# A fused adaLN attention and MLP block on one core: rearranging the prologue and the end of the kernel together

## The chip, the cores and the metric

The kernel runs on one core of one Trainium2 chip. The metric is the device time in microseconds of one execution. Each profile shows one execution; PE is the matrix engine (TensorE), ACT is ScalarE, DVE is VectorE, POOL is GpSimd, SP is SyncE, which only issues DMAs here.

An execution can differ from another by the clock that PE is granted. The trace records it: in the fast executions told here it is 1.00 except in windows of 0.50, whose lengths are multiples of 3.41 us. A run whose time is over 1.5% above the fastest of the same kernel is called slow and left out of comparisons.

## The reference

The inputs are bf16: x is 2048 x 640, there are 32 heads of 20, and the MLP is 1536 wide.

```python
mod = (silu(c) @ w_mod).reshape(1, 6, 1, 640)      # sa, ca, ga, sb, cb, gb
h = layernorm(x) * (1 + ca) + sa
x = x + ga * attention(h, wqkv, wo)                # softmax over 2048 keys
h = layernorm(x) * (1 + cb) + sb
x = x + gb * mlp(h)                                # mlp: layernorm, w1, gelu(tanh), w2
```

## The kernel before

The program is a list of operations, each with an engine, operands, an assumed duration and a priority. A list scheduler in the Python code plays a model of the chip and fixes, before anything runs, the order in which each engine gets its instructions. On the chip each engine takes its instructions strictly in this order. **A changed duration, threshold or DMA estimate in the model therefore changes the order of everything after it.**

The work has three parts. In the prologue the inputs are loaded, x is normalised and transposed, and the first projections are made. In the middle ACT computes 755 exps of 1024 or 1536 columns of scores and one shorter one, PE makes scores and sums, and DVE computes some scores' exps in its own way. Projections, the output projection, the second layer norm and the MLP of earlier query chunks are placed between. In the end the last chunk of 256 tokens does its layer norms and MLP with nothing left to hide behind.

**Filler.** PE is kept busy by matmuls with a zero weight matrix, which change no result. They are put where the modelled PE has a gap and the columns of the last modelled 3.4 to 4.4 us are below a threshold:

```python
class Sched:
    TICK = 3.413
    def __init__(self, nc, es):
        self.fill_min = 4500
        # ...
    def schedule(self):
        # ... bt: when the next PE operation could start, f0: when PE is free
                room = bt > f0 + 0.06
                while room and fl and fl[0][0] < min(bt, f0 + 1.0) - self.TICK:
                    fl.pop(0)
                if burst[1] or room and (bt > f0 + 1.5 and f0 > 30.0 or sum(x[1] for x in fl) < self.fill_min):
                    # ... a filler of up to 512 columns goes to PE
```

**Prologue.** Two small loads for the first head group come from ACT's queue; ACT copies their columns apart; a whole 512-column K block is projected before Q.

```python
for w in (1, 0):
    dma("act", raw0[:, w, :, :], wqkv_v[:, :, w * D:w * D + 80], 102400, prio=0)
dma("sp", wm0[:, :, 0:D], wmod_v[:, :, 0:D], 819200)
# ... stats, rstd (on GpSimd), normalize per token tile, transposes, then
proj_job(0, 1, tc, 0, eng="dve" if tc else "act")       # K
if tc == 0:
    proj_job(0, 0, tc, 0)                               # Q
```

The scheduler marks some operations with `lock`, meaning that GpSimd and DVE may not hold their common SBUF port at once. A GpSimd operation without an input, as a memset is, gets no lock:

```python
def pool(emit, W, R=(), dur=0.2, prio=5, name=""):
    return P.op("pool", emit, R=list(R), W=list(W), dur=dur, lat=dur + 0.12, prio=prio, name=name,
                lock=bool(R))
# ...
pool(lambda e: e.memset(wo_pad, 0.0), [wo_pad], dur=4.4, prio=7)
```

**End.** The softmax sums of the last head group are spread by a selecting matmul to 128 x 256, inverted by DVE in two pieces, and multiplied in. The second layer norm uses DVE for statistics, GpSimd for the inverse root, ACT for the normalise, DVE for the multiply and the add, and the same again for the MLP's own layer norm.

```python
sel_job(ci, NG - 1, prio=1, step=128)   # matmul, then per 128 columns: reciprocal, multiply
# ... last output matmul per half, wo_evac
def ln2(ci, tl, tail=False):
    stats(xt, tt, tl, 3)
    rstd(tt, 1, 1)                       # two GpSimd operations, a third in normalize
    normalize(hd, xt, tt, 3, on_act=tail)
    for op, row in ((ALU.mult, cb1), (ALU.add, sbr)):
        dve(lambda e, op=op, row=row: e.tensor_tensor(hd, hd, row, op=op), ...)
    stats(hd, tt, tl, 3, so=4); rstd(tt, 1, 1, so=4)
    normalize(hd, hd, tt, 3, so=4, on_act=tail)
```

The softmax here doesn't subtract the row's maximum and nothing guards it: scores larger than these inputs give would overflow.

## Time and profile before

| | before |
|---|---|
| timed runs, us | 967.31 median of 3 (966.62 to 972.41) |
| profiled execution, us | 1271.3, granted clock 0.556: a slow one |

The profile was of a slow execution. It shows what waits for what, but not what binds the timed runs.

The first fence is from the page of before: the span, busy time by engine, PE's granted clock in 40 slices (in tenths), the shares of the chain that ended last, and two of the costliest groups (busy us, mean ns, then the idle time before them).

```profile
span 1271.3 us, 17791 instructions
...
PE 1243.1 (98%) x7616; PEld 369.1 (29%) x7676; DVE 706.5 (56%) x1225; ACT 946.8 (74%) x804; POOL 152.0 (12%) x196
...
PEclk6555555555555555555555555555555555555555
...
PE 95%; DVE 3%; issue 1%; ACT 1%; DMA 0%; ACTq 0%
...
L739 ACT ACTIVATE arena<-psum 128x1536 bf16<-128x1536 f32 (+1 forms) x756 | 896.5, 1225 | 255.9 <-PE psum L730 247.2
...
L562 PE MATMUL psum<-arena 128*128 128x512 bf16 (+2 forms) x690 | 254.1, 482 | 0.5 <-issue 0.5
```

Line 739 is the exp, line 562 the filler (690 of them). PE was at about half clock all the time and was the bound of this execution.

The second fence is the timeline of before at its start: start, duration, engine, line, operation, output and input, count, and in brackets the idle time before it and what ended that.

```profile
0.73 3.77 ACTq L471 DMA_DIRECT2D arena<-in_A_wqkv_dram  x2
...
4.52 1.28 ACT L457 ACT_TABLE_LOAD   x1 [4.52 <-DMA arena<-in_A_wqkv_dram]
...
6.03 0.17 DVE L583 CAST arena<-psum 128x5 f32<-128x5 bf16 x1 [4.07 <-ACT arena L457]
...
6.45 0.48 DVE L614 BATCH_NORM_STATS2 arena<-arena 128x6 f32<-128x320 bf16 x1
...
23.61 1.02 ACT L739 ACTIVATE arena<-psum 128x1024 bf16<-128x1024 f32 x1 [1.98 <-PE psum L730]
```

ACT spends its first 4.5 us on issuing two loads, and the statistics of x stand behind ACT's tanh. The first exp starts at 23.61 in this slow execution.

The third is the timeline of before at its end.

```profile
1214.83 0.42 DVE L805 CAST arena<-psum 128x256 bf16<-128x256 f32 x1 [3.76 <-PE psum L797]
...
1216.48 1.77 DVE L816 RECIPROCAL arena<-psum 128x128 f32<-128x128 f32 x2 [1.23 <-PE psum L476]
...
1231.74 1.82 ACT L457 ACTIVATE arena<-arena 128x640 bf16<-128x640 bf16 x2 [3.89 <-POOL arena L628]
```

From the end of the last sums' copy (1215.25) to the end of the second normalised tile (1233.56) are 18.3 us.

### The profile page before, as it was taken

To read this page: it belongs to the slowest core of one execution; us is meant where nothing else is said; L and a number is where in the kernel's file an instruction comes from. 1 tells how busy PE (TensorE), PEld (TensorE's weight loads), DVE (VectorE), ACT (ScalarE), POOL (GpSimd) and SP (SyncE) were. 2 spreads that over 40 slices of the span, in tenths; PEclk is the share of its full clock that TensorE was granted. 3 is DMA by queue.
4 is the path that set the end of the run, shared out by engine and by line. 5 is a ranking of instruction groups with operands and counts; after the bars stand their busy time and mean duration, and the time that the engine had idled before them with its cause. 6 is when DMAs were issued, how large, how long until landed. Compare 5 with 4: busy or idle time off the path is not lost.

```text
span 1271.3 us, 17791 instructions
## 1 busy us (share of the span) xinstructions
PE 1243.1 (98%) x7616; PEld 369.1 (29%) x7676; DVE 706.5 (56%) x1225; ACT 946.8 (74%) x804; POOL 152.0 (12%) x196
## 2 busy tenths in 40 slices
PE   8999999999999999999999999999999999999999
PEld 3423222222222222222222222222233233333345
DVE  6522544554667766766567666666666543666030
ACT  3577777777778777887887877877778786888722
POOL 4200003000001251000013100000033000110010
PEclk6555555555555555555555555555555555555555
DMA  6200001100000030000000000100000000000000
GB/s 224 78 9 1 10 9 61 30 10 9 2 9 9 27 116 9 30 3 18 19 9 10 9 9 9 40 5 16 20 14 10 17 8 16 21 10 10 15 6 11
DMA packets 31521, 30.15 MB, mean 24 GB/s; under 512 B 12882, under 2 KB 26450, under 8 KB 31442
## 3 DMA queue, kind: packets, MB, share of 16 engines
q1 hardware_dynamic: 30130, 28.81, 7.1%
q8 instruction: 60, 0.98, 0.3%
q10 hardware_dynamic: 1312, 0.20, 0.1%
q14 instruction: 19, 0.16, 0.0%
HBM read 26.00 MB, written 2.88 MB: 23 GB/s over the span
## 4 chain that ended last, share of the span: by engine, by line
PE 95%; DVE 3%; issue 1%; ACT 1%; DMA 0%; ACTq 0%
PE psum L476 32%; PE psum L730 23%; PE psum L562 17%; PE psum L797 16%; PE psum L764 4%; PE psum L482 1%; ACT arena L739 1%; DVE arena L632 0%; DVE arena L614 0%; DVE arena L674 0%; DMA arena<-in_A_wqkv_dram 0%; DVE arena L1076 0%; DVE arena L805 0%; DVE arena L679 0%; DVE arena L661 0%
## 5 line engine op out<-in xcount | busy, mean ns | idle before, releaser
L739 ACT ACTIVATE arena<-psum 128x1536 bf16<-128x1536 f32 (+1 forms) x756 | 896.5, 1225 | 255.9 <-PE psum L730 247.2
L476 PE MATMUL psum<-arena 128*128 128x320 bf16 (+4 forms) x1643 | 467.1, 409 | 9.3 <-issue 5.9
L730 PE MATMUL psum<-arena 32*128 32x512 bf16 (+1 forms) x2339 | 380.6, 414 | 9.1 <-issue 5.9
L562 PE MATMUL psum<-arena 128*128 128x512 bf16 (+2 forms) x690 | 254.1, 482 | 0.5 <-issue 0.5
L797 PE MATMUL psum<-arena 128*32 128x512 bf16 (+3 forms) x2560 | 249.4, 415 | 0.6 <-DVE arena L805 0.4
L476 PEld LDWEIGHTS psum<-arena 128*128 128x128 bf16 (+1 forms) x1703 | 154.5, 112 | 239.8 <-issue 176.2
L776 DVE TENSOR_SCALAR arena<-psum 128x512 f32<-128x512 uint16 x176 | 121.5, 690 | 180.6 <-PE psum L764 150.5
L730 PEld LDWEIGHTS psum<-arena 32*128 32x128 bf16 x2339 | 78.9, 92 | 303.7 <-issue 173.7
L841 POOL TENSOR_TENSOR arena<-arena 128x512 bf16<-128x512 bf16 (+1 forms) x39 | 37.9, 973 | 837.1 <-DMA arena<-scr 837.0
L780 DVE SCALAR_TENSOR_TENSOR arena<-arena,psum 128x512 uint16<-128x512 f32 x176 | 120.1, 682 | 25.7 <-PE psum L797 21.7
L777 DVE TENSOR_TENSOR arena<-psum,arena 128x512 f32<-128x512 uint16 x176 | 120.9, 687 | 4.3
L778 DVE SCALAR_TENSOR_TENSOR arena<-psum,arena 128x512 f32<-128x512 uint16 x176 | 120.7, 686 | 3.6
L797 PEld LDWEIGHTS psum<-arena 128*32 128x32 bf16 (+1 forms) x2560 | 53.3, 92 | 178.4 <-issue 170.3
L562 PEld LDWEIGHTS psum<-arena 128*128 128x128 bf16 x690 | 68.2, 113 | 113.0 <-issue 101.1
L764 PE MATMUL psum<-arena 32*128 32x512 bf16 (+1 forms) x221 | 86.1, 423 | 1.9 <-DVE arena L679 0.4
L679 DVE TENSOR_SCALAR arena<-psum,arena 128x512 bf16<-128x512 f32 x31 | 23.2, 749 | 58.1 <-PE psum L476 44.6
L1076 DVE TENSOR_SCALAR arena<-psum,arena 128x512 bf16<-128x512 f32 (+1 forms) x48 | 32.8, 683 | 40.4 <-PE psum L476 38.5
L1097 DVE TENSOR_TENSOR arena<-psum,arena 128x320 bf16<-128x320 f32 x32 | 15.6, 489 | 64.0 <-PE psum L476 61.1
L674 DVE TENSOR_SCALAR arena<-psum,arena 128x512 bf16<-128x512 f32 x32 | 24.0, 751 | 45.1 <-PE psum L476 36.8
L805 DVE CAST arena<-psum 128x512 bf16<-128x512 f32 (+1 forms) x40 | 23.3, 584 | 44.7 <-PE psum L797 44.4
L614 DVE BATCH_NORM_STATS2 arena<-arena 128x6 f32<-128x320 bf16 x96 | 44.2, 478 | 0.3
L1056 POOL TENSOR_TENSOR arena<-arena 128x640 bf16<-128x640 bf16 x28 | 39.0, 1395 | 22.6 <-DVE arena L632 21.6
(54 smaller groups left out, 276.1 us busy)
## 6 DMA issues: line engine op xcount, KB each, us to landing
arena<-scr SPq DMA_DIRECT2D x24, 256.0 KB
arena<-in_A_x_dram SPq DMA_DIRECT2D x6, 640.0 KB, 11.5
arena<-in_B_w_dram SPq DMA_DIRECT2D x2, 1920.0 KB, 13.4
arena<-in_w_mod_dram SPq DMA_DIRECT2D x2, 1600.0 KB
out_dram<-arena SPq DMA_DIRECT2D x16, 160.0 KB, 1.8
arena<-in_A_wqkv_dram SPq DMA_DIRECT2D x3, 800.0 KB
arena<-scr SPq DMA_DIRECT2D x15, 128.0 KB
arena<-in_w_mod_dram SPq DMA_DIRECT2D x2, 800.0 KB
```

Source lines behind the costliest of these rows:

```text
L476: return P.op("pe", lambda e: e.matmul(outp, lhsT, rhs, start=start, stop=stop), R=[lhsT, rhs], W=[outp], dur=d, lat=d + 0.17, prio=prio, ...
L562: return lambda e: e.matmul(bank(b_)[:, 0:n_], zero, r_, start=new, stop=new, skip_group_check=True)
L614: dve(lambda e, hf=hf, xi=xi: e.bn_stats(s6[:, hf, :], xi), [xi], [s6[:, hf, :]], 320, prio=prio, dur=0.39)
L730: r = e.matmul(o_, lh, rh, start=True, stop=True, tile_position=(32 * hl, 0))
L739: acts.append(P.op("act", lambda e: e.activation(dst, pb, ACTF.Exp, scale=ESC, bias=EBIAS), R=[pb], W=[dst], dur=d, lat=d + 0.24, prio=4, ...
L764: r = e.matmul(o_, lh, rh, start=True, stop=True, tile_position=(32 * hl, 0))
L776: dve(lambda e: e.tensor_scalar_add(w_, m_, -65536.0), [pb], [w_], w, prio=1, name="d1", dur=0.6)
L777: dve(lambda e: e.tensor_tensor(w_, m_, w_, op=ALU.mult), [pb, w_], [w_], w, prio=1, name="d2", dur=0.6)
L778: dve(lambda e: e.scalar_tensor_tensor(out=w_, in0=m_, scalar=c2, in1=w_, op0=ALU.add, op1=ALU.mult), [pb, w_], [w_], w, prio=1, name="d3" ...
L780: dve(lambda e: e.scalar_tensor_tensor(out=o_, in0=w_, scalar=al, in1=pb, op0=ALU.mult, op1=ALU.add), [w_, pb], [o_], w, prio=1, name="d4" ...
L797: r = e.matmul(o_, lh, rh, start=(kt == 0), stop=(kt == TT - 1), tile_position=(0, 32 * hl))
L1056: pool(lambda e, op=op, row=row: e.tensor_tensor(hd, hd, row, op=op), [hd], [hd, row], dur=1.4)
```

## The change

The change starts the first exp earlier and shortens the end. The diff, cut to its core:

```diff
@@ scheduler
-        self.fill_min = 4500
+        self.fill_min = 5000
+        self.fill_all = 16.0
-                if burst[1] or room and (bt > f0 + 1.5 and f0 > 30.0 or sum(x[1] for x in fl) < self.fill_min):
+                if burst[1] or room and (bt > f0 + 1.5 and f0 > 30.0 or f0 < self.fill_all
+                                         or sum(x[1] for x in fl) < self.fill_min):
-                s = max(bt + 1.4, bw)
-                bw = s + o.nbytes / 350e3
-                o.t1 = bw + 0.6
+                big = o.nbytes > 65536
+                s = max(bt + (2.0 if big else 1.4), bw)
+                bw = s + o.nbytes / (330e3 if bt < 20.0 else 350e3)
+                o.t1 = bw + (1.6 if big else 0.6)
@@ prologue
-        for w in (1, 0):
-            dma("act", raw0[:, w, :, :], wqkv_v[:, :, w * D:w * D + 80], 102400, prio=0)
         dma("sp", wm0[:, :, 0:D], ...)
         dma("sp", wm0[:, :, D:2 * D], ...)
+        for w in (1, 0):
+            dma("sp", raw0[:, w, :, :], wqkv_v[:, :, w * D:w * D + 80], 102400)
-            act(dst, src, ACTF.Copy, n=400, prio=1)
+            pool(lambda e, dst=dst, src=src: e.tensor_copy(dst, src), [dst], [src], dur=0.5, prio=1)
-                    ["act", "dve", "dve"] if tc else ["act", "dve", "act"])      # who evacuates transposes
+                    ["act", "dve", "dve"])
-            proj_job(0, 1, tc, 0, eng="dve" if tc else "act")
             if tc == 0:
-                proj_job(0, 0, tc, 0)
+                proj_job(0, 1, 0, 0, eng="act", part=(0, 128))
+                proj_job(0, 0, 0, 0)
+                proj_job(0, 1, 0, 0, eng="act", part=(128, 512))
+            else:
+                proj_job(0, 1, tc, 0)
@@ end
+        act(rsm[:, 16:17], kcol[:, 0:1], ACTF.Sqrt, n=1, prio=9, name="table")
-        sel_job(ci, NG - 1, prio=1, step=128)
+        inv_tail(ci, NG - 1, inv, bankh(4))
+        #   transpose ot to token-major, reciprocal of its 8 sum columns, split the result in two bf16
+        #   parts, and spread them back with 16 small matmuls against the identity
-            ln2(ci, tl, tail=True)
+        a, b = (ln2_tail(ci, tl) for tl in range(nt))
+        #   one fixed DVE order (each operation follows the one before):
+        #   stats; ACT sqrt; (x - m) * cb1; reciprocal; x * r + sbr; stats; ACT sqrt; reciprocal; normalise
+        act(rsm[:, 17:18], ..., ACTF.Gelu_apprx_tanh, n=1, prio=2, name="table")
```

The rise of the filler threshold from 4500 to 5000 holds for the whole kernel.

## The prediction

> **What bounds the kernel now.** Timed median 967.31 us. The profiled execution is a slow one: span 1271.3 us, granted clock 0.556 (cores view), PE busy 98%, chain of waits 95% PE; so it shows the order of work, not the bound of the timed runs. At that clock 512 columns take 0.40 us back to back though PE never rests; the Trainium skill ("TensorE: Matmul & The Clock Gate", Part 1) says that a busy PE is released to full clock: this trace disagrees. At full clock I estimate PE work at 1243 x 0.556 = 690 us, so the timed runs should be bound by ScalarE: 947 us busy on the page, neighbours overlapping by some 0.1 us (three 1024-wide exps took 2.97, one alone 1.02). With 755 exps that leaves 870 to 910 us from first exp to last, and about 58 us for prologue and end. Only these two change.
>
> **Prologue.** First exp at 23.6 us (timeline). The chain of waits begins with two loads issued from ScalarE's queue (0.73 to 4.50), then the table load (1.28), tanh, and VectorE's small cast at 6.03, behind which the statistics stand until 6.45. The change issues these loads from SyncE, later. Statistics can start when x lands, about 4.5: 2 us. ScalarE evacuates two transposed tiles instead of three (3 took 2.11): 0.6 us. Only 128 columns of K before Q: 5 x 384 columns off the path to the first score, 0.8 us at full clock. Filling all PE gaps before 16 us (PE busy 2.16 of 4 in 8 to 12) may spare half-clock projections: 0 to 1.5 us. The weight copies move to GpSimd, off the path if their loads land by 11. Sum 4; perhaps 3 reach the end, since ScalarE still waits on other work up to 60 us.
>
> **End.** From the sums' copy (ends 1215.25) to the second normalised tile (1233.56): 18.3 us, estimated 16.3 at full clock (28 early output matmuls held PE). Now: two 128-column reciprocals (0.93 each), divides, per tile statistics, three GpSimd steps (0.22 + 0.55 + 0.27), ScalarE normalise (0.92), multiply and add (0.48 each), and statistics to normalise again. The change: reciprocal of 8 columns, two small ops, two short PE passes: 1 us less. The layer norms become one VectorE order: 4 evacuations 0.42, 8 statistics 0.42, 4 aggregates 0.12, 4 reciprocals 0.15, 4 fused scalar-tensor-tensor at (640 + 151)/0.96 = 0.82 (formula of "VectorE: DVE Perf Modes", errata section; the trace's 0.489 at 320 columns agrees), 2 normalises 0.4: 10.5, plus 1.8 before: 12.3. Gain 4. Tables (1.28 each) load ahead: at most 0.5, since PE bounds the following matmuls. Transposes, MLP and store (about 25 us at full clock) stay.
>
> **Sum.** 967.3 - 3 - 4.5 = 959.8 us; 80% range 953 to 965.5. Faster by over 2% (below 948): 0.05. Within 2%: 0.93. Slower: 0.02.
>
> **Signs.** Right: first statistics near 4.5, first exp at least 3 us earlier; 12 to 13 us from the sums' copy to the second normalised tile; no GpSimd in the end; exps unchanged. Wrong: GpSimd's copies or the late loads release the first K projection; fused ops over 0.9 us; a table load on the chain; first to last exp grows by what the prologue saved.
>
> **What would make it wrong.** More filler (5000 columns a window) delaying exps in the middle; a half-clock end in the timed runs too, where surplus fillers (20 us here) enlarge the saving; the early start absorbed before 60 us.

## The result, and the profile after

| | before | after |
|---|---|---|
| timed runs, us | 966.96 median of 4 (966.22 to 972.41) | 981.53 median of 4 (981.0 to 982.03) |
| ratio of fast runs | | 1.0138, 95% interval 1.0101 to 1.0176 |

A ratio is the mean time of one kernel's fast runs over that of the other's fast runs of the same rounds, so it is not quite the ratio of the medians. The kernel became 1.4% slower where I had predicted 0.8% faster. The interval lies wholly above 1.

The profile of after is of a fast execution. The same parts of its page:

```profile
span 979.2 us, 18273 instructions
...
PE 956.1 (98%) x7888; PEld 346.5 (35%) x7888; DVE 701.7 (72%) x1233; ACT 916.1 (94%) x807; POOL 149.8 (15%) x186
...
PEclk9799999999999999999999999999999999999999
...
PE 86%; ACT 8%; DVE 5%; issue 0%; POOL 0%; POOLq 0%; DVEq 0%
...
L747 ACT ACTIVATE arena<-psum 128x1536 bf16<-128x1536 f32 (+1 forms) x756 | 865.5, 1237 | 21.9 <-PE psum L738 16.0
...
L575 PE MATMUL psum<-arena 128*128 128x512 bf16 (+2 forms) x878 | 232.0, 357 | 0.0
```

Even at full clock the chain is 86% PE, and there are 878 fillers where there were 690. One slice has clock 7. What this has to be compared with is the chain of before, profiled later (before_fast), and its filler line:

```profile
ACT 45%; PE 42%; DVE 6%; DMA 3%; issue 1%; POOL 1%; SPq 0%; DVEq 0%
...
L562 PE MATMUL psum<-arena 128*128 128x512 bf16 (+2 forms) x690 | 177.1, 351 | 0.2 <-issue 0.2
```

So in fast executions the chain went from ACT and PE in about equal parts to nearly PE alone, and the filler's busy time from 177.1 to 232.0 us. The timeline of after at its start:

```profile
0.72 1.28 ACT L465 ACT_TABLE_LOAD   x1 [0.72 <-PEq L1288]
...
3.06 1.28 ACT L465 ACT_TABLE_LOAD   x1
...
4.91 1.67 DVE L627 BATCH_NORM_STATS2 arena<-arena 128x6 f32<-128x320 bf16 x4
...
17.74 1.28 ACT L747 ACT_TABLE_LOAD   x1
...
19.04 1.94 ACT L747 ACTIVATE arena<-psum 128x1024 bf16<-128x1024 f32 x2
```

The statistics start at 4.91, as predicted. There are two table loads more than expected (without the dummy square root, in after_no_table, only the one at 0.72 is left before the first exp). The dummy square root, meant to load a table ahead of the end, depends on nothing late. The scheduler put it at 4.70 us, and so the exp table had to be loaded again at 17.74, right before the first exp. The timeline at its end:

```profile
946.41 0.42 DVE L813 CAST arena<-psum 128x256 bf16<-128x256 f32 x1 [2.98 <-PE psum L805]
...
947.42 0.21 DVE L822 RECIPROCAL arena<-psum 128x8 f32<-128x8 bf16 x1 [0.59 <-PE psum L495]
...
952.16 0.88 DVE L1104 SCALAR_TENSOR_TENSOR arena<-arena 128x640 bf16<-128x640 bf16 x1
...
960.25 0.45 DVE L639 TENSOR_SCALAR arena<-arena 128x640 bf16<-128x640 bf16 x1
```

From the copy's end (946.83) to the second tile's end (960.70) are 13.9 us.

### The profile page after: what moved, and what is told of

Same layout as the page of the kernel before. It is cut to its first block, busy times and chain, and to the rows that moved or that the text cites. A ratio compares the mean times of both kernels' runs of the same rounds, so it can differ in the third digit from the quotient of the medians.

```text
span 979.2 us, 18273 instructions
## 1 busy us (share of the span) xinstructions
PE 956.1 (98%) x7888; PEld 346.5 (35%) x7888; DVE 701.7 (72%) x1233; ACT 916.1 (94%) x807; POOL 149.8 (15%) x186
## 4 chain that ended last, share of the span: by engine, by line
PE 86%; ACT 8%; DVE 5%; issue 0%; POOL 0%; POOLq 0%; DVEq 0%
PE psum L489 27%; PE psum L738 22%; PE psum L575 16%; PE psum L805 15%; ACT arena L747 6%; PE psum L772 4%; ACT arena L1140 1%; PE psum L495 1%; DVE arena L639 1%; DVE arena L627 1%; DVE arena L784 1%; ACT L747 1%; ACT L1140 0%; DVE arena L813 0%; DVE arena L668 0%
## 5 line engine op out<-in xcount | busy, mean ns | idle before, releaser
L747 ACT ACTIVATE arena<-psum 128x1536 bf16<-128x1536 f32 (+1 forms) x756 | 865.5, 1237 | 21.9 <-PE psum L738 16.0
L489 PE MATMUL psum<-arena 128*128 128x320 bf16 (+5 forms) x1708 | 345.0, 307 | 4.7 <-ACT arena L1140 1.2
L738 PE MATMUL psum<-arena 32*128 32x512 bf16 (+1 forms) x2339 | 301.8, 341 | 4.1 <-ACT arena L747 3.5
L575 PE MATMUL psum<-arena 128*128 128x512 bf16 (+2 forms) x878 | 232.0, 357 | 0.0
L805 PE MATMUL psum<-arena 128*32 128x512 bf16 (+3 forms) x2560 | 204.4, 345 | 1.3 <-DVE arena L813 1.2
L489 PEld LDWEIGHTS psum<-arena 128*128 128x128 bf16 x1708 | 130.5, 97 | 158.0 <-issue 94.0
L738 PEld LDWEIGHTS psum<-arena 32*128 32x128 bf16 x2339 | 76.9, 91 | 202.2 <-issue 101.3
L575 PEld LDWEIGHTS psum<-arena 128*128 128x128 bf16 x878 | 72.4, 98 | 95.4 <-issue 68.1
L772 PE MATMUL psum<-arena 32*128 32x512 bf16 (+1 forms) x221 | 67.4, 337 | 3.6 <-DVE arena L788 2.8
L687 DVE TENSOR_SCALAR arena<-psum,arena 128x512 bf16<-128x512 f32 x31 | 23.2, 749 | 27.5 <-PE psum L489 27.2
L1081 POOL TENSOR_TENSOR arena<-arena 128x640 bf16<-128x640 bf16 x28 | 39.1, 1397 | 14.8 <-DVE arena L639 13.7
L682 DVE TENSOR_SCALAR arena<-psum,arena 128x512 bf16<-128x512 f32 x32 | 23.9, 748 | 19.4 <-PE psum L489 19.3
```

Source lines behind the costliest of these rows:

```text
L489: return P.op("pe", lambda e: e.matmul(outp, lhsT, rhs, start=start, stop=stop), R=[lhsT, rhs], W=[outp], dur=d, lat=d + 0.17, prio=prio, ...
L575: return lambda e: e.matmul(bank(b_)[:, 0:n_], zero, r_, start=new, stop=new, skip_group_check=True)
L738: r = e.matmul(o_, lh, rh, start=True, stop=True, tile_position=(32 * hl, 0))
L747: acts.append(P.op("act", lambda e: e.activation(dst, pb, ACTF.Exp, scale=ESC, bias=EBIAS), R=[pb], W=[dst], dur=d, lat=d + 0.24, prio=4, ...
L772: r = e.matmul(o_, lh, rh, start=True, stop=True, tile_position=(32 * hl, 0))
L805: r = e.matmul(o_, lh, rh, start=(kt == 0), stop=(kt == TT - 1), tile_position=(0, 32 * hl))
```

## The experiments

Two theories were stated first. **A:** the added fillers take PE time that scores need. **B:** the loss is in the prologue. As rivals, **C** says that the changed model merely gave the middle another, worse order. After the first runs **D** was added: one memset on GpSimd holds DVE. Its rival **E** puts the lost time of the prologue down to other order, DMA or the weight copies. Sixteen experiments ran; all gave the right result. They ran in batches on different chips (numbers 12, 3, 12 and 8 in order of time), with before in each batch; ratios are within a batch.

To place a loss, I read the start times of the 756 exps from each trace. The table shows the profiled run of each kernel, in us: when the first and the 41st exp start; the stretch from the 61st to the 551st exp; the end, from the last exp's end to the last instruction; and the time at half clock in the whole span. The fillers in the stretch are counted. Half clock after the last instruction is left out. The median is of all timed runs of that kernel; profiles and times of single runs spread, so a few tenths of a microsecond at the first exp are not read as effects.

| kernel | 1st exp | 41st exp | 61st to 551st | fillers in it | end | half clock | median |
|---|---|---|---|---|---|---|---|
| before_fast | 19.8 | 69.4 | 580.5 | 330 | 35.5 | 23.9 | 970.51 (one run) |
| after | 19.0 | 76.9 | 590.0 | 451 | 33.6 | 10.5 | 981.53 |
| after_fill4500 | 19.0 | 76.8 | 580.6 | 325 | 33.5 | 17.1 | 968.03 |
| before_fill5000 | 18.9 | 68.9 | 589.5 | 451 | 35.5 | 0.0 | 980.08 |
| after_no_table | 18.4 | 77.2 | 590.0 | 451 | 33.5 | 10.2 | 981.23 |
| after_thin | 19.2 | 77.4 | 581.0 | 451 | 33.3 | 51.2 | 982.35 |
| end_only | 19.3 | 68.9 | 580.0 | 330 | 33.7 | 13.7 | 967.81 |
| f4500_memset | 19.0 | 68.4 | 579.2 | 325 | 33.6 | 10.2 | 960.28 |
| f4500_memset_notable | 17.6 | 67.7 | 581.6 | 325 | 33.5 | 13.7 | 960.55 |
| f4500_split | 18.9 | 68.6 | 579.1 | 325 | 33.5 | 3.4 | 959.45 |
| after_memset | 18.8 | 68.6 | 590.1 | 452 | 33.5 | 10.5 | 975.76 |
| f4750_memset | 19.3 | 68.9 | 582.6 | 388 | 33.6 | 0.6 | 961.62 |
| f4000_memset | 19.5 | 68.7 | 575.7 | 228 | 33.3 | 11.1 | 955.32 |
| f3500_memset | 19.7 | 68.7 | 578.8 | 163 | 37.0 | 37.5 | 964.94 |
| f2500_memset (slow profile) | 19.3 | 71.2 | 602.2 | 96 | 45.1 | 205.7 | 995.71 |
| before_f4000 | 23.0 | 76.4 | 580.7 | 229 | 35.8 | 61.4 | 975.92 |
| f4000_split_notable | 20.0 | 69.8 | 575.7 | 228 | 38.5 | 32.5 | 963.41 |

### Before in the fast state

The edit is none.

> The kernel before, unchanged, for a profile of the fast state. All theories: about 967 us, clock near 0.995. From first exp to last I expect about 909 us, against 926.6 in the profile of after; if it is 920 or more instead, the loss lies in the prologue or the end and not in the middle.

Measured: 970.51 us in one run, clock 0.988. From first exp to last end 913.2 us against 926.6, so the loss was in the middle, but not evenly. The 41st exp of before starts at 69.4, that of after at 76.9: 7.5 us are lost before it. The stretch from the 61st to the 551st, at full clock in both, takes 9.5 us longer in after. These two are separate losses. Later this run of before has 20.5 us at half clock, which fits its being some 4 us longer than its median of 966 to 967.

The next two fences are the view of busy time in the stretch 100 to 690 us, before_fast first, then after. The columns are the window, its length, busy us and count for PE, PE's weight loads, DVE, ACT and GpSimd, then the clock, the DMA share and GB/s.

```profile
100.00:690.00 590.00, 562.43 (x3955) 180.19 (x3994) 475.76 (x777) 584.66 (x505) 88.86 (x91) 1.00 0.08 26
```

```profile
100.00:690.00 590.00, 583.26 (x4055) 184.87 (x4055) 462.33 (x757) 580.60 (x497) 87.72 (x90) 1.00 0.08 26
```

ACT looks 98 to 99% busy in both, so by this view alone ACT binds both. But in the same time after does 497 ACT instructions and before 505, and PE's busy time rises from 95% to 99%. How both can be true is seen between neighbouring exps. Over the 490 steps of the stretch a next exp starts on average 124 ns before the one before it ends in before_fast, and only 93 ns before in after (a step without overlap counts as zero). An exp whose scores come just as the one before it ends leaves no idle time on ACT; it only overlaps less. The later ones do leave some: in the stretch 39 exps of before_fast waited for PE's scores with ACT idle, 5.2 us in all, and 84 exps of after, 9.3 us.

### The threshold, both ways

```diff
 # after_fill4500, from after
-        self.fill_min = 5000
+        self.fill_min = 4500
```

> After with the filler threshold back at 4500 (654 fillers instead of 878). Theory A (filler in the middle takes PE time from the scores, about 220 x 0.21 = 47 us of PE work): about 957 us, the middle 15 us or more shorter. Theory B (the loss comes from the prologue: half-clock window at 33 to 44 us and the extra table load): still about 980 us. Theory C (the static schedule was merely re-timed): anything between, with no relation to the filler count.

Measured: 968.03 us, ratio to before 1.0004 (0.9966 to 1.0043). The stretch is back to 580.6 us, as A says. But A expected 957 us, and the 41st exp still starts at 76.8. So with the old threshold the change gives nothing: something else in it costs as much as its prologue and end gain.

```diff
 # before_fill5000, from before
-        self.fill_min = 4500
+        self.fill_min = 5000
```

> Before with only the filler threshold raised to 5000 (903 fillers instead of 690). Theory A: slower by 15 to 22 us, about 985 us. Theory B: no change, 967 us. Theory C: within 5 us of 967 either way.

Measured: 980.08 us, ratio 1.0129 (1.0073 to 1.0184); stretch 589.5, 451 fillers. This one line does to before nearly all that the whole change did to the total. The extra fillers did what they were for: the profiled run has no half-clock window. They cost more than the windows did.

### The dummy square root

```diff
 # after_no_table, from after
-        act(rsm[:, 16:17], kcol[:, 0:1], ACTF.Sqrt, n=1, prio=9, name="table")
```

> After without the dummy square root that was meant to load the table ahead of the end but runs at 4.7 us and forces the exp table to be loaded again at 17.74. Theory A: about 1.3 us gained in the prologue, 980 us. Theory B: up to 5 us gained. No theory expects the end to get longer by more than 0.5 us, as the compiler puts the table load straight after the last exp anyway.

Measured: 981.23 us, no change. The first exp starts 0.6 us earlier, and the end is not longer. The 41st exp is not earlier (77.2 against 76.9), so the reload at 17.74 is covered by what holds ACT later. The expected 1.3 us did not come.

### The same order with thin fillers

Lowering the threshold also changes the order of other instructions. To tell filler time from order, this kernel keeps every instruction of after in its place and only makes every fourth filler 32 columns wide.

```diff
 # after_thin, from after
         def filler(b_, n_, new):
+            nfill[0] += 1
+            if nfill[0] > 88 and nfill[0] % 4 == 0:
+                n_ = 32
```

> After with every instruction in the same order on every engine, but every fourth filler past the prologue 32 columns wide instead of up to 512 (about 198 of 878, some 40 us of PE time). Theory A (filler takes PE time): 966 to 971 us, the stretch from the 41st exp to the last 855 to 860 us against 867.6. Theory C (the other order costs it): 978 us or more.

Measured: 982.35 us. By the total both the expected 966 to 971 of A failed and C's 978 or more came. The stretches tell another story. From the 61st to the 551st exp, with no half-clock window in either, the thin kernel takes 581.0 us against 590.0, with the same 451 fillers in the same order. So 9.0 of the 9.5 us are the columns of the fillers, not the order. Counted in the traces, the fillers of the stretch have 228,416 columns in after, 176,864 in after_thin and 167,616 in before_fast (580.5 us): with nearly as few columns as before, the order of after is nearly as fast as before. Behind the 551st exp this kernel falls into half-clock windows of 27.3, 3.4 and 10.2 us, which after does not have there, and 551st to last takes 267.5 us against 255.6. The mean clock shows it (view of cores: span, granted clock), thin first, then after:

```profile
core 0: 982.4 us, clock 0.974
```

```profile
core 0: 979.2 us, clock 0.995
```

So the filler has a price and a use, and this run shows both. The stretch is the clean comparison; the total is not.

### The lost prologue: a memset on GpSimd

The timeline of after around 27 to 35 us:

```profile
27.60 4.36 POOL L1036 MEMSET arena<- 128x5120 bf16 x1
...
28.56 3.58 DVE L639 TENSOR_SCALAR arena<-arena 128x640 bf16<-128x640 bf16 x1
...
32.99 0.73 DVE L687 TENSOR_SCALAR arena<-psum,arena 128x512 bf16<-128x512 f32 x1
...
33.78 0.39 PE L495 MATMUL psum<-arena 128*128 128x128 bf16 x2 [2.80 <-DVE arena L687]
...
34.75 1.02 ACT L747 ACTIVATE arena<-psum 128x1024 bf16<-128x1024 f32 x1 [3.30 <-PE psum L738]
```

And of before_fast:

```profile
27.46 1.23 DVE L632 TENSOR_SCALAR arena<-arena 128x640 bf16<-128x640 bf16 x2
...
28.45 4.54 POOL L1007 MEMSET arena<- 128x5120 bf16 x1
...
29.58 0.69 DVE L679 TENSOR_SCALAR arena<-psum,arena 128x512 bf16<-128x512 f32 x1
...
30.98 1.02 ACT L739 ACTIVATE arena<-psum 128x1024 bf16<-128x1024 f32 x1 [1.46 <-PE psum L730]
```

A normalise of 640 columns takes 0.45 us where nothing disturbs it. In after it starts 1 us after the memset and ends just after it, 3.58 us later. Behind it in DVE's order stands the evacuation of K (L687), for which PE and then ACT wait. PE idles 2.80 us, and from 33.5 us on it gets half clock for 10.24 us. In before_fast the same normalise, the tenth of 16, starts at 27.92, half a microsecond before the memset, and is done at 28.69; nothing is held for long. The scheduler could not see the collision, since a memset has no lock in its model.

The change did not invent this collision. It stands in the slow profile of before that lay open for the prediction, where the ninth normalise takes 4.03 us of the second line (two normalises):

```profile
31.53 4.36 POOL L1007 MEMSET arena<- 128x5120 bf16 x1
...
32.04 4.38 DVE L632 TENSOR_SCALAR arena<-arena 128x640 bf16<-128x640 bf16 x2
```

The same kernel has it in its slow execution and not in its fast one. after_fill4500, after_no_table and after_thin have it as after does (4.31, 4.31 and 4.12 us for the tenth normalise).

The Trainium skill ("GPSIMD Engine Reference", section 8, Key points) says that GpSimd "Shares its SBUF interfaces with VectorE — contention with DVE instructions in a 2-port perf mode or with two SBUF inputs". The trace agrees as far as it goes: the normalise (one SBUF input and output, bf16) is held, while statistics (0.43 to 0.49 us) and evacuations from PSUM (0.69 for L679) run at their usual length beside the memset of before_fast. That the normalise runs in a 2-port mode is not shown; that its 640 columns take 0.45 us, where the fused operations of the end take 0.83 to 0.89 for as many, fits a faster mode.

```diff
 # f4500_memset, from after_fill4500
                     normalize(hn1[...], x_[:, tl, :], 4 * tc + tl, 3)
+                    last_norm = P.ops[-1]
-        pool(lambda e: e.memset(wo_pad, 0.0), [wo_pad], dur=4.4, prio=7)
+        P.op("pool", lambda e: e.memset(wo_pad, 0.0), W=[wo_pad], dur=4.4, lat=4.52, prio=7, after=(last_norm,))
```

> After with the threshold at 4500 and the 10 KB memset on GpSimd (4.36 us, started at 27.60) held back until the last normalise of the prologue. Theory D (the memset holds VectorE's normalise for 3.5 us, PE then idles 2.8 us and runs 10.2 us at half clock): the 41st exp starts at 69 to 70 us instead of 76.8, total about 960 us. Theory E (the prologue lost its time by other order, DMA or weight copies): 41st exp still after 75 us, total 966 to 968.

Measured: 960.28 us, ratio to before 0.9936 (0.9884 to 0.9989). The 41st exp starts at 68.4. D predicted 69 to 70 and about 960; E predicted 75 or more and 966 to 968. The tenth normalise is free again:

```profile
28.36 0.43 DVE L639 TENSOR_SCALAR arena<-arena 128x640 bf16<-128x640 bf16 x1
```

```diff
 # f4500_split, from after_fill4500: same release, eight pieces
+                    if tc == 1:
+                        norm7 = P.ops[-1]          # the eighth normalise
-        pool(lambda e: e.memset(wo_pad, 0.0), [wo_pad], dur=4.4, prio=7)
+        for g in range(NG):
+            wg = wo_pad[:, g, :]
+            P.op("pool", lambda e, wg=wg: e.memset(wg, 0.0), W=[wg], dur=0.55, lat=0.67, prio=7, after=(norm7,))
```

> After with the threshold at 4500 and the memset cut into eight pieces of 640 columns (about 0.55 us each), released by the same event as the one memset was. Theory D (one long GpSimd instruction holds VectorE's normalise until it ends): no normalise between 20 and 40 us takes over 1.2 us, 41st exp at 68 to 71 us, total 960 to 962. If what costs is GpSimd's total time or the place of the memset in the order: a normalise or a wait of 3 us stays, total 966 to 968.

Measured: 959.45 us, ratio 0.9912 (0.9861 to 0.9964), 41st exp at 68.6. The timeline of f4500_split at the same place:

```profile
28.07 0.62 POOL L1040 MEMSET arena<- 128x640 bf16 x1
...
28.30 0.58 DVE L639 TENSOR_SCALAR arena<-arena 128x640 bf16<-128x640 bf16 x1
```

The normalise meets a piece of the memset at the same moment of the program and takes 0.58 us. So it is the length of one GpSimd instruction that held DVE, not GpSimd's total work nor its place. (A later pair, at 31.58, took 1.29 for two beside a run of three pieces.)

```diff
 # f4500_memset_notable, from f4500_memset
-        act(rsm[:, 16:17], kcol[:, 0:1], ACTF.Sqrt, n=1, prio=9, name="table")
```

> The same, also without the dummy square root in the prologue: first exp at 18.4 instead of 19.0; total 0.5 to 1.3 us below f4500_memset if ScalarE is the bound from there on, the same if PE or DMA is.

Measured: 960.55 us, no gain, though its 41st exp is at 67.7 and its first at 17.6. The profiled run has 13.7 us at half clock against 10.2, and 6.8 of them in the stretch. What 0.7 us are worth here is below what these runs can tell.

```diff
 # after_memset, from f4500_memset
-        self.fill_min = 4500
+        self.fill_min = 5000
```

> After with its threshold of 5000, only the memset moved behind the last normalise. If the two losses add up: 981.5 less 7.5 to 8 = about 973.5 us; 41st exp at 68 to 69 us; exps 61 to 551 still 589 to 590 us. If the filler loss depended on the bad start: 960 to 966.

Measured: 975.76 us, ratio 1.0072 (1.0026 to 1.0118); 41st exp at 68.6, stretch 590.1. The two losses add up within 2 us.

### The end alone

```diff
 # end_only, from before
+        the end of after: inv_tail, div_tail, ln2_tail, the Gelu table load; no dummy square root
```

> Before with the end of after alone (inverse sums as columns, one VectorE order for the layer norms, tables), all of the prologue and the threshold as before. I expect the end, from the last exp's end, at 33.5 us against 35.5, and a total of about 964.5 us, 2 us below before. If the end gains the 4.5 us that I predicted, 962.

Measured: the end takes 33.7 us against 35.5; it is 33.3 to 33.6 in the kernels with the new end and a threshold of 4500 or more, and in f4000_memset. The total is 967.81 us, ratio 1.0011 (0.9947 to 1.0076). Its runs spread from 963.37 to 973.7 us with clocks from 0.993 to 0.980, so a gain of 2 us is inconclusive by the total.

The two lines that bound the end in before_fast's timeline are these:

```profile
933.68 0.42 DVE L805 CAST arena<-psum 128x256 bf16<-128x256 f32 x1 [2.92 <-PE psum L797]
...
948.11 1.82 ACT L457 ACTIVATE arena<-arena 128x640 bf16<-128x640 bf16 x2 [3.89 <-POOL arena L628]
```

From 934.10 to 949.93 are 15.8 us, against 13.9 in after.

### How much filler is right

All from f4500_memset (or before), only `self.fill_min` changed to the number in the name.

> Threshold 4750, memset moved (757 fillers against 653 at 4500 and 875 at 5000). Theory A, filler columns cost in proportion: exps 61 to 551 in about 584 us, total about 965 us with fewer half-clock windows than at 4500.

Measured: 961.62 us, ratio 0.9929 (0.9886 to 0.9972), stretch 582.6, almost no half clock. The expectation of 584 and 965 was a little too high.

> Threshold 4000, memset moved (479 fillers). Theory A alone would give some 945 to 955 us; but if fillers are what keeps PE out of half-clock windows, there will be many of these, clock under 0.98 and 965 us or more. I expect the second, with the stretch between windows no faster than at 4500, as ScalarE binds there.

Measured: 955.32 us, ratio to before 0.9873 (0.9823 to 0.9924), stretch 575.7. My expectation failed twice. The stretch became faster still, so ACT's exps were not the only bound at 4500, and the half-clock windows stayed few (11.1 us in the profiled run). In its chain ACT leads clearly:

```profile
ACT 63%; PE 28%; DVE 7%; DMA 1%; issue 1%; SPq 0%; DVEq 0%
```

A next exp now starts 162 ns before its predecessor ends (counted as above). This is the fastest kernel. Its four runs lie between 954.25 and 960.42 us. From 4500 to 4000 the order changes too, and no kernel here holds it fixed.

> Threshold 3500 (400 fillers against 479). If filler still costs in proportion: exps 61 to 551 in about 574 us where the clock is full, and more half-clock windows; total 953 to 960. If ScalarE binds from here: the stretch stays at 575 to 576.

Measured: 964.94 us, ratio 0.9964 (0.989 to 1.0037); 37.5 us at half clock, 10.2 of them in the stretch, which takes 578.8. Whether the stretch would be faster at full clock stays open.

> Threshold 2500 (284 fillers). I expect the half-clock windows to outweigh: clock below 0.97, total above 965 us. If filler is of no use at all, 950.

Measured: 995.71 us, ratio 1.0261 (1.0182 to 1.0339), clocks 0.916 to 0.925 in the fast runs. Here the windows outweigh by far (in its slow profile 95.6 us at half clock lie in the stretch alone).

> Before with the threshold at 4000 alone: exps 61 to 551 in 575 to 577 us against 580.5, total 961 to 963 us, that is 6 to 8 above f4000_memset, which has the rearranged prologue and end as well (2 us from the end, 1 to 2 from the prologue, the rest fewer half-clock windows).

Measured: 975.92 us, ratio 1.0076 (1.0002 to 1.015). I expected 961 to 963. The profiled run was at half clock for 10.2 us from 10.8 us on, where before has 3.4, and its first exp starts at 23.0. Then the memset meets a normalise here too: the ninth takes 3.16 us beside it, from 29.89 on. Together they bring the 41st exp to 76.4. In the kernels with the rearranged prologue, which fills every PE gap before 16 us, no half-clock window lay before the first exp in any profile. This may be a use of that part of the change at a lower threshold, but no kernel has it alone, and before_fill5000 has no such window either. The 20 us between before_f4000 and f4000_memset, larger than the 6 to 8 that I expected, are in the profiled runs 7.7 up to the 41st exp, 4.9 in the stretch, 4.2 behind it and 2.5 in the end. So a good third of them is the prologue, with the memset in it, and the rest goes with 61.4 against 11.1 us at half clock.

```diff
 # f4000_split_notable, from f4500_split
-        self.fill_min = 4500
+        self.fill_min = 4000
-        act(rsm[:, 16:17], kcol[:, 0:1], ACTF.Sqrt, n=1, prio=9, name="table")
```

> Best so far by the runs: after with threshold 4000, the memset in eight pieces, without the dummy square root. 953 to 956 us; first exp near 18.

Measured: 963.41 us, ratio 0.9954 (0.9892 to 1.0016). The stretch is 575.7 as in f4000_memset, but 30.7 us at half clock fell on the time after 730 us, and the end took 38.5 us against 33.3, nearly all at full clock. Of the 7.9 us between the two profiled spans 5.2 are this end and only 1.6 lie between the 551st and the last exp, where the window is. There PE's order has 33 matmuls in 4.95 us, most of them for an earlier chunk's MLP, where f4000_memset has 4 in 0.72, and the last layer norm waits for them. So here the order costs more than the windows do. f3500_memset has the same 33 and an end of 37.0 us. The two runs at 4000 were on different chips, which no run here separates from the order; 955.32 is a measured time of one order, not a promise for its neighbours.

## Why the prediction was right or wrong

It was wrong in the sign of the total: 981.53 us for a predicted 959.8, range 953 to 965.5.

**The step that failed first: "Only these two change", with "the timed runs should be bound by ScalarE".** I scaled PE's busy time of the slow profile by its clock (1243 x 0.556 = 690 us) and concluded that PE had a quarter of its time free. On the fast page of before PE is busy 916.8 us (177.1 of them filler), not 690, and in the middle 562.43 of 590. A score matmul that took a mean of 0.41 us on the slow page takes 0.34 on the fast one, not 0.23, so PE's busy time does not scale with its clock; why not, no run shows. PE and ACT bind together in before (42% and 45% of the chain), PE alone in after (86%), and the filler is not free. The threshold was a term of zero in my sum. Measured, it is 9.5 us between the 61st and the 551st exp alone, shown from both sides (after_fill4500, before_fill5000) and with the order held (after_thin). I had named it among what would make the prediction wrong and gave it no size.

**The second: "perhaps 3 reach the end" from the prologue.** The mechanism at the very start was right: statistics at 4.91 (predicted 4.5), 5.95 in before_fast. But the first exp came 0.8 us earlier than in before_fast, not 3, partly by the table load at 17.74, 1.28 us on the path: without the dummy square root it came 1.4 us earlier than there. Even this may be much for the new prologue: before_fill5000, with the old prologue but no half-clock window in it, starts its first exp at 18.9, as early as after. Then 7.5 us were lost up to the 41st exp. The memset that the change does not touch met a normalise that it had just missed. Moved away, the 41st exp starts at 68.4, against 69.4 in before_fast and 68.9 in before_fill5000 and end_only, which have the old prologue. So what the prologue gives at that point is 0.5 to 1 us, not 3.

**The end: mechanism right, size off.** Predicted 4.5 us; the whole end gave 1.9 (35.5 to 33.6). From the copy to the second tile the gain was predicted as 16.3 less 12.3 and measured as 15.8 less 13.9. The mis-sized terms are two. The steps before the first evacuation took 2.6 us (946.83 to 949.43) for 1.8 predicted, and the layer norms 11.3 for 10.5. In the latter eight statistics took 4.0 us for 3.4 predicted; why they take longer here, no run shows. The fused operations were sized well: 0.83 to 0.89 us for an estimate of 0.82. The estimate applies the formula (N + 151)/0.96 ns, which the Trainium skill ("VectorE: DVE Perf Modes", errata section) gives for an fp32 tensor_tensor add, to these fused bf16 operations of 640 columns; that it carries over is what this trace shows, not the page. The 0.5 us hoped for from tables was not there: from the second tile to the last instruction are 18.5 us in both after and before_fast.

**Signs.** Of my signs for "wrong" one came true as written, "a table load on the chain": the load at 17.74 lies on after's chain of waits for 1.28 us, though its removal gained nothing in the total. "First to last exp grows by what the prologue saved" came true only in half: it grew from 913.2 to 926.6 us, far more than the 0.8 us by which the first exp came earlier. Of the signs for "right" the statistics and GpSimd's absence from the end came; the 3 us at the first exp and the 12 to 13 us in the end (13.9) did not.

**Luck.** f4500_memset, the change without the two losses, takes 960.28 us, close to the predicted 959.8. That is not the prediction come true: its prologue gives 0.5 to 1 us for 3 and its end 1.9 for 4.5. In the profiled runs 5.5 of the 9.9 us by which its span is under before_fast's lie behind the 551st exp, where before_fast has 20.5 us at half clock and f4500_memset 10.2.

The sum, from the two profiled runs: 7.5 (up to the 41st exp) + 0.3 (41st to 61st) + 9.5 (61st to 551st) - 4.6 (551st to the last, where before_fast has 20.5 us at half clock) - 1.9 (the end) = 10.8 us, for spans of 979.2 and 968.5. The timed medians differ by 14.6, as the profiled before was some 4 us over its median.

## What to carry to other kernels

In a statically scheduled kernel a local change is not local: read the middle again, by the start times of the same instruction in both traces, before crediting the part that was edited. Filler that keeps the clock up costs what the engine's next real work is delayed by, so it must be priced where that engine is near its bound. Its best amount is found by measuring both losses: here 9.4 us for 126 fillers too many (after against after_fill4500), and some 25 us over before, in fast runs, for a threshold far too low. Cut long GpSimd instructions into pieces, or keep them away from DVE operations like this normalise, since one can hold everything in DVE's order behind it. And look in the profile for one short operation that took ten times its usual length: here it stood in the profile of before.

## What the Trainium skill lacked or had wrong

- "TensorE: Matmul & The Clock Gate", Part 1, describes a half clock for an idle PE and a full one for a busy PE, decided in windows of about 3.4 us. The fast traces agree (1.00 or 0.50 only, windows of 3.41 us and multiples). The profiled slow execution of before does not: clock 0.556 through 1271.3 us with PE busy 98% (its clock records are 0.555 and 0.50, none is 1.00). What held it there no run shows.
- The same page, "Why this matters for your kernels", advises no idle gaps over about 3 us. In after 10.24 us at half clock began within a gap of 2.80 us, that is a shorter one. The page has no advice on what filler costs: going from 325 to 452 fillers in 490 exps cost 10.9 us (579.2 to 590.1), while 228 to 325 cost 3.4.
- "GPSIMD Engine Reference", section 8, names the contention but not its length; elsewhere the skill is not silent on that. Here a memset of 4.36 us, which has no SBUF input, stretched a normalise to 3.58 us; beside pieces of 0.62 us it took 0.58.
- "ScalarE: Activation LUTs", What ACT_TABLE_LOAD costs, gives an overlap of about 93 ns between back-to-back activations. Here it is not one number: the mean over the stretch, with late starts counted as zero, was 93 ns in after, 124 in before_fast and 162 in f4000_memset, so it grew as filler was taken away. Its 1283 ns for a table load agrees with the 1.28 us seen.
